# A position bias from an unscaled table: the maximum takes the constant, the eviction gives it back

## The chip, the cores and the metric

The kernel runs on one core of one Trainium2 chip. The metric is device time in microseconds (us), from repeated executions on the same chip; a further execution was recorded by the hardware profiler, and all rows below come from that one. The engines are TensorE (PE; PEld for its weight loads), VectorE (DVE), ScalarE (ACT), GpSimd (POOL) and SyncE (SP), which issues the DMAs.

## The reference

Attention with a learned relative-position bias, and two feed-forward layers behind it. Cut to what the change touches:

```python
pos = np.arange(S)                                        # S = 576
rel = (pos[:, None] - pos[None, :]).astype(np.float32)
psi_rel = np.log1p(np.abs(rel))
psi_i = np.log1p(np.maximum(pos[:, None].astype(np.float32), 1.0))
x = (psi_rel / psi_i)[..., None]
h = np.maximum(x @ w1 + b1, 0.0)                          # 32 hidden units
bias = h @ w2                                             # 8 heads
scores = scores + bias.transpose(2, 0, 1)[None, :, :, :]
# softmax, values; then silu(x @ w_gate) * (x @ w_val) @ w_out, then softplus(x @ w_in) @ w_out
```

psi_i is positive, so max(psi_rel / psi_i * w1 + b1, 0) = max(psi_rel * w1 + b1 * psi_i, 0) / psi_i. Both kernels use this: the inner maximum is computed per hidden unit, multiplied by w2, and the division by psi_i (with the factor 8 of the score scale) is done when the result is evicted.

## The kernel before

The program has three parts, one behind the other: the bias stage, attention, and the two feed-forward layers. The first is the one that the change touches.

**Table.** One input, `G`, holds 128 rows (32 hidden units for each of four row groups): the columns `wb_sb` (w1 and b1 of the row's hidden unit), `W2` (w2 laid out for four groups of rows), `PB` (psi_i, 36 slabs x 4 parts), a near and a far table of log-distances, and `inv` (8 / psi_i for each slab). It comes in two DMAs: everything up to the near table, then the far table and `inv`.

**Slabs.** The bias of 576 rows x 576 columns x 8 heads is made in 36 slabs; `order` says that slabs 32 to 35 (near table) come first, then 0 to 31 (far table). For one slab `hidden` makes four tiles `r` of 128 x 576, one per part `ct`: a window of the table, plus the part's bias, and the maximum with 0. Three are made by VectorE (one instruction with an add and a maximum, L267), the fourth by ScalarE (a Relu with a bias, L265). In the first slab two of the four are made by ScalarE, straight from the unscaled table with w1 as scale (L261). `second` multiplies the four tiles by `W2` on TensorE into a PSUM tile `pb` of 128 x 576 (eight matmuls of 288 columns, one per part and half, L275). `keep` evicts it with ScalarE, times `inv`, into a staging tile (L287), and SyncE sends it to its place in `bias` (L291, L294).

**Scaling.** Before the slabs VectorE multiplies `PB` by b1 in place (L604) and the near table by w1 into a tile `N` (L605); ScalarE multiplies the far table by w1 in place (L607).

**Order.** PE, ACT, DVE, POOL and SP run each in the order in which the code issues (a manual schedule). `hidden` runs two slabs ahead of `second`; there are 12 `r` tiles (three slabs) and two `pb` tiles. After slabs 23, 26, 31 and 33 (`EARLY`) the first attention chunks are run between slabs: two or four score matmuls (L311), a score-plus-bias with a row minimum on VectorE (L359), an exponential on ScalarE (L373). All other attention chunks stand behind the last slab. Ten warm-up matmuls (L602) stand ahead of the first slab on TensorE.

Of the kernel before, what the change touches and what calls it, by code (L numbers as in the profile page):

```python
# [11 lines left out]
F32 = mybir.dt.float32  # L12
F32R = mybir.dt.float32r
I32 = mybir.dt.int32
AF = mybir.ActivationFunctionType
ALU = mybir.AluOpType
# [3 lines left out]
P = 128  # L20
B, H, S, D, HID = 2, 8, 576, 64, 32
# [28 lines left out]
HALF = S // 2  # L50
# [3 lines left out]
GU0, GW = 487, 487 + S + 1  # L54
TU0, TW = 563, 51 + S + 1
# [48 lines left out]
def tile_kernel(ctx: ExitStack, tc, qT, kT, vS, vT, wg, wv, wo, wi, wo2, table, out):  # L104
    nc = tc.nc
# [11 lines left out]
    def slots(pool, tag, names):  # L117

        for name in names:
            n = len([1 for t in SLOTS.values() if t[0] == tag])  # L120
            SLOTS[name] = (tag, [pool.tile([P, 2, S], F32R, tag=f"{tag}{2 * n + i}", name=f"{name}{t}") for i, t in enumerate("hl")])

    def opener(stack):
        return lambda name, bufs, **k: stack.enter_context(
            tc.tile_pool(name=name, bufs=bufs, reuse_waits="tile", **k)
        )

    rctx = ExitStack()
    with ExitStack() as actx:
        pool = opener(actx)  # L130
        biasp = pool("biasp", 1)
        bias = [biasp.tile([P, H, S], F32, name=f"bias{c}") for c in range(2)]
# [19 lines left out]
        def new_pairs(name, count, pool=pool, **k):  # L152

            ep = pool(name, 1, **k)
            for _ in range(count):
                pairs.append(ep.tile([P, 2 * S], F32, name=f"e{len(pairs)}"))
            return ep
# [5 lines left out]
        psS = pool("psS", 2, space=PSUM)  # L163
# [73 lines left out]
        gp = pool("gp", 1)  # L237
# [1 line left out]
        psB = pool("psB", 2, space=PSUM)  # L239

        G = gp.tile([P, 34 + 144 + TW + GW + 36], F32, name="G")
        N = gp.tile([P, TW], F32, name="N")
        near = 34 + 144
        cut = near + TW
        sp.dma_start(out=G[:, :cut], in_=table[:, :cut])
        sp.dma_start(out=G[:, cut:], in_=table[:, cut:])
        wb_sb, W2, PB, inv = G[:, :2], G[:, 2:34], G[:, 34:near], G[:, cut + GW :]

        def hidden(i):
            s = order[i]  # L250
            c, t = divmod(s, 8)
            rs = []
            for ct in range(4):
                if c < 4:
                    src, w0 = G, cut + GU0 - (P * c + 32 * ct + t)
                else:
                    src, w0 = N, TU0 - (P * c + 16 * ct + t)
                r = rp.tile([P, S], F32, name="r")
                n = 4 * s + ct
                if i == 0 and ct > 1:  # L260
                    nc.scalar.activation(  # L261
                        r, G[:, near + w0 : near + w0 + S], AF.Relu, bias=PB[:, n : n + 1], scale=wb_sb[:, 0:1]
                    )
                elif ct == 3:
                    nc.scalar.activation(r, src[:, w0 : w0 + S], AF.Relu, bias=PB[:, n : n + 1])  # L265
                else:
                    nc.vector.tensor_scalar(r, src[:, w0 : w0 + S], PB[:, n : n + 1], 0.0, op0=ALU.add, op1=ALU.max)  # L267
                rs.append(r)
            return rs

        def second(rs):
            pb = psB.tile([P, 2, 512], F32, tag="B", name="pb")
            for hf in range(2):
                for ct in range(4):
                    nc.tensor.matmul(  # L275
                        pb[32 * ct : 32 * ct + 32, hf, :HALF],
                        W2,
                        rs[ct][:, HALF * hf : HALF * (hf + 1)],
                        start=True,
                        stop=True,  # L280
                    )
            return pb

        def keep(s, pb):
            c, t = divmod(s, 8)
            st = next(staging)
            nc.scalar.activation(  # L287
                st.rearrange("p (a n) -> p a n", a=2), pb[:, :, :HALF], AF.Copy, scale=inv[:, s : s + 1]
            )
            if c < 4:  # L290
                sp.dma_start(out=bias[c][t : t + 121 : 8], in_=st)  # L291
            else:
                for a in range(2):
                    sp.dma_start(out=bias[c][D * a + t : D * a + t + 61 : 4], in_=st[a::2])  # L294
# [304 lines left out]
        with tc.manual_schedule(engines={E.PE, E.Activation, E.DVE, E.Pool, E.SP}):  # L599
            warm = psS.tile([P, 2, 512], F32, tag="S", name="warm")  # L600
            for _ in range(WARM):
                nc.tensor.matmul(warm[:, 0, :P], ident, ident, start=True, stop=True)  # L602

            nc.vector.tensor_scalar(PB, PB, wb_sb[:, 1:2], None, op0=ALU.mult)  # L604
            nc.vector.tensor_scalar(N, G[:, near:cut], wb_sb[:, 0:1], None, op0=ALU.mult)  # L605
            hid = [hidden(i) for i in range(2)]
            nc.scalar.mul(G[:, cut : cut + GW], G[:, cut : cut + GW], wb_sb[:, 0:1])  # L607
            for i, s in enumerate(order):
                pb = second(hid.pop(0))
                if i + 2 < len(order):  # L610
                    hid.append(hidden(i + 2))
                keep(s, pb)
                if i in EARLY:
                    run_slot()
            sctx.close()
            slots(xp, "a", ("B11", "T1"))
            pool = opener(actx)
            ep1 = new_pairs("ep1", 4, opener(right), side="right")
            tmpp = pool("tmpp", 1)
            t2f = tmpp.tile([P, 2, S], F32, name="t2f")  # L620
            for i, mp in enumerate((tmpp, ep1)):
                mixes.append(mp.tile([P, 5 * P], F32, name=f"m{i}"))
                nc.gpsimd.memset(mixes[-1][:, S:], 0.0)
            atp = pool("atp", 6)
            fp = pool("fp", 1)
            psT = pool("psT", 3, space=PSUM)
            psO = pool("psO", 1, space=PSUM)
            while slot < len(chunks) or jobs or turned or gathered or done or late or waiting:
                run_slot()
# [447 lines left out]
    with tc.manual_schedule(engines={E.PE}):  # L1077
        quads = {"z": z}
        for q in range(4):
# [5 lines left out]
            for word in f"{OTHER if q else FIRST} {TAIL}".split():  # L1085
                who, what = word
                if who in "tu":
                    n = int(what)
                    if ws is None:
                        ws = convert(first + 2, outs[0]) + convert(first + 3, outs[1])  # L1090
                    if q == 3 and n == 4:
                        t = TOKENS[n][0]
                        a = acc[t // 2][:, t % 2]
                        for at in (slice(0, DM // 2), slice(DM // 2, DM)):
                            if who == "t":
                                held[n, at.start] = wide()[:, 0]
                            ps = held[n, at.start]
# [9 lines left out]
                    for i, t in enumerate(TOKENS[n]):  # L1107
                        if who == "t":
                            continue
                        a, ps = acc[t // 2][:, t % 2], held[n][:, i]  # L1110
# [57 lines left out]
```

## Time and profile before

| | |
|---|---|
| median of 3 runs | 587.25 us (587.23 to 587.41) |
| profiled execution | 587.23 us |
| its span, first to last instruction | 585.5 us |
| busy, share of the span | PE 98%, PEld 86%, DVE 78%, ACT 64%, POOL 17% |
| mean granted TensorE clock | 1.00 |

Busy shares are averages over stages with different limits. The bias stage takes roughly the first tenth of the span; which engine is full there is read from a view of that stage alone. A busy time that includes overlap counts an instruction from its start to its end, though the next may start earlier, so a pace is read from start to start.

### The profile page before, as it was taken

What the parts mean: (1) busy time and instruction counts of PE and PEld (TensorE: products, weight loads), DVE (VectorE), ACT (ScalarE), POOL (GpSimd) and SP (SyncE); (2) the same over time, 40 slices, a digit from 0 to 9 for tenths busy, and PEclk for the clock granted to TensorE, in tenths of its full rate; (3) what the DMA queues carried; (4) which work ended last, traced back from release to release, by engine and by line L of the source; (5) the groups of instructions that cost most, each with busy time, mean ns of one, the idle gap of its engine ahead of it and who ended that gap; (6) DMA issues with size and microseconds to landing.
All of it is one profiled execution on the core that took longest, in us unless ns stands there. A gap on an engine that the chain in (4) does not pass through costs nothing.

```text
span 585.5 us, 11330 instructions
## 1 busy us (share of the span) xinstructions
PE 574.0 (98%) x4282; PEld 504.9 (86%) x4282; DVE 454.4 (78%) x971; ACT 375.1 (64%) x713; POOL 99.1 (17%) x151
## 2 busy tenths in 40 slices
PE   8999999999999999999999999999999999999997
PEld 5334588888887999999999999999989989988986
DVE  7999688888988998977879626579998876983432
ACT  7999888888787857656567325359726725733520
POOL 1002578888871000000000000000000000000000
PEclk9999999999999999999999999999999999999999
DMA  8999633233233342332343231322254241310012
GB/s 314 214 208 214 153 100 118 85 107 113 72 112 112 103 143 73 109 109 73 108 129 126 72 109 45 104 99 69 86 160 123 74 143 28 118 36 1 2 50 112
DMA packets 42039, 63.32 MB, mean 108 GB/s; under 512 B 4096, under 2 KB 30976, under 8 KB 41984
## 3 DMA queue, kind: packets, MB, share of 16 engines
q1 hardware_dynamic: 41984, 62.59, 36.2%
q8 instruction: 34, 0.56, 0.4%
q14 instruction: 21, 0.17, 0.1%
HBM read 49.60 MB, written 2.36 MB: 89 GB/s over the span
## 4 chain that ended last, share of the span: by engine, by line
PE 85%; DVE 6%; ACT 5%; DMA 2%; POOL 1%; issue 1%; DVEq 0%; POOLq 0%; ACTq 0%
PE pw L756 38%; PE pw L1064 17%; PE pw L707 13%; PE po L437 6%; PE pt L410 4%; PE ps L338 4%; ACT early L287 2%; ACT r L265 2%; PE ps L311 2%; PE pb L275 2%; DVE e L359 1%; DMA bias<-early 1%; DVE r L267 1%; DVE bias L359 1%; DVE T1l L457 1%
## 5 line engine op out<-in xcount | busy, mean ns | idle before, releaser
L1064 PE MATMUL pw<-oh,g2h 128*128 128x512 f32 (+1 forms) x148 | 56.9, 384 | 0.0
L1064 PE MATMUL pw<-oh,g2l 128*128 128x512 f32 (+1 forms) x148 | 56.9, 384 | 0.0
L1064 PE MATMUL pw<-ol,g2h 128*128 128x512 f32 (+1 forms) x148 | 56.8, 384 | 0.0
L707 PE MATMUL pw<-gl,sh 128*128 128x384 f32 x144 | 48.2, 335 | 0.0
L707 PE MATMUL pw<-gh,sl 128*128 128x384 f32 x144 | 48.2, 334 | 0.0
L707 PE MATMUL pw<-gh,sh 128*128 128x384 f32 x144 | 48.2, 334 | 0.0
L681 DVE SCALAR_TENSOR_TENSOR x<-raw,x 128x512 int32<-128x512 int32 x68 | 46.2, 687 | 0.9
L275 PE MATMUL pb<-r,G 128*32 128x288 f32 x576 | 42.7, 412 | 4.0 <-ACT early L287 1.4
L383 POOL TENSOR_SCALAR e<-e,sm 128x576 f32<-128x576 f32 x44 | 34.2, 788 | 65.2 <-DVE sm L380 49.0
L267 DVE TENSOR_SCALAR r<-G 128x576 f32<-128x576 f32 x96 | 42.0, 517 | 0.0
L359 DVE CUSTOM_DVE_ANT_0 e<-ps,bias 128x576 f32<-128x576 f32 x44 | 33.0, 750 | 11.5 <-PE ps L338 6.5
L275 PEld LDWEIGHTS pb<-r,G 128*32 128x32 f32 x576 | 16.8, 109 | 28.9 <-ACT early L287 17.1
L417 ACT COPY at<-pt 128x512 f32<-128x512 f32 (+2 forms) x69 | 36.4, 549 | 6.5 <-PE pt L410 6.1
L338 PE MATMUL ps<-kst,ql 128*128 128x288 f32 x120 | 36.9, 336 | 1.4 <-DVE sm L377 0.6
L437 PE MATMUL po<-at,v 128*64 128x256 f32 (+3 forms) x384 | 37.2, 332 | 1.0 <-DVE at L417 0.8
L373 ACT ACTIVATE e<-e,sm 128x576 f32<-128x576 f32 x44 | 34.3, 781 | 3.5 <-DVE sm L359 3.1
L678 DVE TENSOR_SCALAR x<-x 128x512 int32<-128x512 int32 x68 | 28.7, 427 | 9.4 <-ACT x L677 5.2
L1114 DVE TENSOR_TENSOR acc<-pw,acc 128x512 f32<-128x512 f32 x26 | 16.8, 684 | 23.7 <-PE pw L1064 23.7
L437 PEld LDWEIGHTS po<-at,v 128*64 128x64 f32 x384 | 26.8, 137 | 8.5 <-issue 1.7
L1064 PEld LDWEIGHTS pw<-oh,g2l 128*128 128x128 f32 x148 | 27.8, 188 | 5.7
L1064 PEld LDWEIGHTS pw<-ol,g2h 128*128 128x128 f32 x148 | 27.8, 188 | 5.1
L1064 PEld LDWEIGHTS pw<-oh,g2h 128*128 128x128 f32 x148 | 27.8, 188 | 5.0
(274 smaller groups left out, 1677.9 us busy)
## 6 DMA issues: line engine op xcount, KB each, us to landing
raw<-in_wo_dram SPq DMA_DIRECT2D x28, 512.0 KB, 3.4
bias<-early SPq DMA_DIRECT2D x32, 288.0 KB, 7.5
raw<-in_wi_dram SPq DMA_DIRECT2D x16, 512.0 KB, 4.1
raw<-in_wv_dram SPq DMA_DIRECT2D x12, 512.0 KB, 4.5
raw<-in_wg_dram SPq DMA_DIRECT2D x12, 512.0 KB, 3.5
qr<-in_qT_dram SPq DMA_DIRECT2D x7, 576.0 KB, 3.8
bias<-in_kT_dram SPq DMA_DIRECT2D x6, 576.0 KB, 4.5
v<-in_vS_dram SPq DMA_DIRECT2D x8, 384.0 KB, 3.3
```

The lines of the kernel that those rows point to most:

```text
L267: nc.vector.tensor_scalar(r, src[:, w0 : w0 + S], PB[:, n : n + 1], 0.0, op0=ALU.add, op1=ALU.max)
L275: nc.tensor.matmul(pb[32 * ct : 32 * ct + 32, hf, :HALF], W2, rs[ct][:, HALF * hf : HALF * (hf + 1)], start=True, stop=True,)
L338: nc.tensor.matmul(ps[:, hf, :HALF], u[t][:, o : o + P], kst[:, a, HALF * hf : HALF * (hf + 1)], start=i == 0, stop=i == len(parts) - 1,)
L359: nc.vector.tensor_tensor_reduce(out=e[:, :S].rearrange("p (a n) -> p a n", a=2), in0=ps[:, :, :HALF], in1=bt.rearrange("p (a n) -> p a n" ...
L373: nc.scalar.activation(e, e, AF.Exp, bias=sm[:, 0, n : n + 1], scale=-1.0, accum_out=u["sums"][:, n, :1])
L383: nc.gpsimd.tensor_scalar(e, e, sm[:, 2, i : i + 1], 1.0, op0=ALU.mult, op1=ALU.mult)
L417: marks[eng, u["i"], u["sub"]] = copy(at[:, :w], pt[:, :w]).ins
L437: nc.tensor.matmul(u["po"][D * a : D * (a + 1), o : o + n], v[:, D * t : D * (t + 1)], at[:, i : i + n], start=piece == 0 and o == 0, stop ...
L681: nc.vector.scalar_tensor_tensor(yi, lw, 29, yi, op0=ALU.logical_shift_right, op1=ALU.bitwise_or)
L707: nc.tensor.matmul(ps[:, :n], w[:, k], x, start=first and k == 0 and i == 0, stop=last and k == NK - 1 and i == 2)
L756: nc.tensor.matmul(ps[:, hf, :HALF], a[:, o + k], b[:, HALF * hf : HALF * (hf + 1)], start=start and k == 0 and i == 0, stop=k == 1 and i ...
L1064: nc.tensor.matmul(ps[:, at], g, w.rearrange("p k f -> p (k f)")[:, at], start=f == 0 and i == 0, stop=f == 3 and i == 2)
```

## The change

The table is no longer scaled ahead of the slabs. With a table entry g and a part's bias b = b1 * psi_i, the kernel before computes max(g * w1 + b, 0). The changed kernel computes max(g * w1, -b) in VectorE for three of the parts, which is smaller by b; the missing b, multiplied by `W2` and `inv`, is added in the eviction. `floor` holds -b for the three parts and 0 for the fourth; `edge` holds b for the fourth, whose Relu on ScalarE takes bias and scale. `shifts` multiplies `floor` by `W2` in four matmuls of 36 columns and turns the result into `shift`, one number per row and slab, which becomes the bias of the eviction (now Identity with a bias and a scale instead of Copy with a scale). The tile `N`, the scaling of both tables and the special case of the first slab are gone.

```diff
         G = gp.tile([P, 34 + 144 + TW + GW + 36], F32, name="G")
-        N = gp.tile([P, TW], F32, name="N")
+        floor = gp.tile([P, 36, 4], F32, name="floor")
+        edge = gp.tile([P, 36], F32, name="edge")
+        shift = gp.tile([P, 36], F32, name="shift")
...
+        PB = G[:, 34:near].rearrange("p (s c) -> p s c", c=4)
+        nc.gpsimd.memset(floor[:, :, 3], 0.0)
 
         def hidden(i):
...
                 r = rp.tile([P, S], F32, name="r")
-                n = 4 * s + ct
-                if i == 0 and ct > 1:
-                    nc.scalar.activation(
-                        r, G[:, near + w0 : near + w0 + S], AF.Relu, bias=PB[:, n : n + 1], scale=wb_sb[:, 0:1]
-                    )
-                elif ct == 3:
-                    nc.scalar.activation(r, src[:, w0 : w0 + S], AF.Relu, bias=PB[:, n : n + 1])
+                g, w1 = G[:, w0 : w0 + S], wb_sb[:, 0:1]
+                if ct == 3:
+                    nc.scalar.activation(r, g, AF.Relu, bias=edge[:, s : s + 1], scale=w1)
                 else:
-                    nc.vector.tensor_scalar(r, src[:, w0 : w0 + S], PB[:, n : n + 1], 0.0, op0=ALU.add, op1=ALU.max)
+                    nc.vector.tensor_scalar(r, g, w1, floor[:, s, ct : ct + 1], op0=ALU.mult, op1=ALU.max)
                 rs.append(r)
             return rs
+
+        def shifts():
+
+            ps = psS.tile([P, 2, 512], F32, tag="S", name="ps")
+            for ct in range(4):
+                nc.tensor.matmul(ps[32 * ct : 32 * ct + 32, 0, :36], W2, floor[:, :, ct], start=True, stop=True)
+            nc.vector.scalar_tensor_tensor(shift, ps[:, 0, :36], -1.0, inv, op0=ALU.mult, op1=ALU.mult)
...
             nc.scalar.activation(
-                st.rearrange("p (a n) -> p a n", a=2), pb[:, :, :HALF], AF.Copy, scale=inv[:, s : s + 1]
+                st.rearrange("p (a n) -> p a n", a=2),
+                pb[:, :, :HALF],
+                AF.Identity,
+                bias=shift[:, s : s + 1],
+                scale=inv[:, s : s + 1],
             )
...
-            nc.vector.tensor_scalar(PB, PB, wb_sb[:, 1:2], None, op0=ALU.mult)
-            nc.vector.tensor_scalar(N, G[:, near:cut], wb_sb[:, 0:1], None, op0=ALU.mult)
+            nc.vector.tensor_scalar(
+                floor[:, :, :3], PB[:, :, :3], wb_sb[:, 1:2], -1.0, op0=ALU.mult, op1=ALU.mult
+            )
+            nc.scalar.mul(edge, PB[:, :, 3], wb_sb[:, 1:2])
             hid = [hidden(i) for i in range(2)]
-            nc.scalar.mul(G[:, cut : cut + GW], G[:, cut : cut + GW], wb_sb[:, 0:1])
+            shifts()
             for i, s in enumerate(order):
```

ScalarE's queue from its first table instruction on, in the kernel before (`r` are the hidden tiles, `early` the staging tiles of the eviction, `pb` the PSUM tile of a slab):

```order
L261 ACTIVATE r<-G 128x576 x2
L265 ACTIVATE r<-N,G 128x576
L607 ACTIVATE G<-G 128x1064
L265 ACTIVATE r<-N,G 128x576
L287 ACTIVATE early_120<-pb,G 128x576
L265 ACTIVATE r<-N,G 128x576
L287 ACTIVATE early_120<-pb,G 128x576
```

Two Relus with bias and scale, one Relu, the scaling of the far table and one more Relu stand ahead of the first eviction there. The same place in the changed kernel, where `edge` and `shift` are the new operands:

```order
L620 ACTIVATE edge<-G 128x36
L267 ACTIVATE r<-G,edge 128x576 x3
L296 ACTIVATE early_120<-pb,shift,G 128x576
L267 ACTIVATE r<-G,edge 128x576
L296 ACTIVATE early_120<-pb,shift,G 128x576
L267 ACTIVATE r<-G,edge 128x576
```

The scaling of the table and one Relu are gone from ahead of the first eviction, and the small `edge` stands first; Relu and eviction alternate as before. VectorE's queue from its start to the first attention chunk, in the kernel before (`e` is that chunk's score tile):

```order
L604 TENSOR_SCALAR G<-G 128x144
L605 TENSOR_SCALAR N<-G 128x628
L267 TENSOR_SCALAR r<-N,G 128x576 x11
L267 TENSOR_SCALAR r<-G 128x576 x66
L359 ISA e_115,sm_100<-ps,bias_71 128x576
```

Two scalings stand ahead of 77 maxima. The same place in the changed kernel:

```order
L617 TENSOR_SCALAR floor<-G 128x36x3
L269 TENSOR_SCALAR r<-G,floor 128x576 x6
L278 SCALAR_TENSOR_TENSOR shift<-ps,G 128x36
L269 TENSOR_SCALAR r<-G,floor 128x576 x72
L372 ISA e_115,sm_100<-ps,bias_71 128x576
```

One small instruction (`floor`) stands ahead of 78 maxima, and the shift stands behind the sixth of them, where it waits for TensorE's four small products. On TensorE these four stand between the warm-up matmuls and the first slab. The order of the DMAs on SP is the same.

## Rows read from the trace of the kernel before

**Rows 1.** The page's chain that ended last, share of the span by engine.

```profile
PE 85%; DVE 6%; ACT 5%; DMA 2%; POOL 1%; issue 1%; DVEq 0%; POOLq 0%; ACTq 0%
```

**Rows 2.** Chain of waits in order of time: start us, us, what.

```profile
55.11 0.74 ACT early L287
...
188.50 126.71 PE pw L756 x960
```

**Rows 3.** Busy time of each engine in two stretches of the bias stage.

```profile
core 0: us, PE busy (x) PEld busy (x) DVE busy (x) ACT busy (x) POOL busy (x), PEclk, DMA share, GB/s
...
9.00:37.00 28.00, 25.52 (x352) 9.15 (x352) 28.00 (x67) 28.00 (x44) 0.00 (x0) 1.00 1.03 235
37.00:57.00 20.00, 18.92 (x228) 8.67 (x220) 18.59 (x50) 19.50 (x34) 2.83 (x5) 1.00 1.05 213
```

**Rows 4.** Timeline of ScalarE: start us, us, engine line op out<-in xcount [idle before].

```profile
4.24 1.62 ACT L261 ACTIVATE r<-G 128x576 f32<-128x576 f32 x2 [2.23 <-DVE G L604]
...
5.78 0.76 ACT L265 ACTIVATE r<-N,G 128x576 f32<-128x576 f32 x1
...
6.44 1.17 ACT L607 ACTIVATE G<-G 128x1064 f32<-128x1064 f32 x1
...
8.18 0.72 ACT L287 ACTIVATE early<-pb,G 128x576 f32<-128x576 f32 x1
8.81 0.76 ACT L265 ACTIVATE r<-N,G 128x576 f32<-128x576 f32 x1
...
37.88 0.83 ACT L287 ACTIVATE early<-pb,G 128x576 f32<-128x576 f32 x1
```

**Rows 5.** Timeline of VectorE from its start to the first attention chunk.

```profile
3.91 0.30 DVE L604 TENSOR_SCALAR G<-G 128x144 f32<-128x144 f32 x1 [3.91 <-DMA G<-in_table_dram]
4.12 0.54 DVE L605 TENSOR_SCALAR N<-G 128x628 f32<-128x628 f32 x1
4.70 4.81 DVE L267 TENSOR_SCALAR r<-N,G 128x576 f32<-128x576 f32 x11
9.43 28.43 DVE L267 TENSOR_SCALAR r<-G 128x576 f32<-128x576 f32 x66
```

**Rows 6.** Timeline of TensorE: two slabs at the start, two later (half-matmuls counted).

```profile
5.94 2.21 PE L275 MATMUL pb<-r,G 128*32 128x288 f32 x32
...
41.97 2.15 PE L275 MATMUL pb<-r,G 128*32 128x288 f32 x32
```

**Rows 7.** Relus of L261 and L265: duration ns min/median/max, first and last start.

```profile
L261 ACT ACTIVATE r<-G x2: 852/860/867, 4.2 to 5.0; 128x576 f32<-128x576 f32 x2
...
L265 ACT ACTIVATE r<-N,G x3: 759/760/762, 5.8 to 8.8; 128x576 f32<-128x576 f32 x3
```

**Rows 8.** Timeline of ScalarE in the feed-forward part: casts and copies without operands.

```profile
305.77 1.25 ACT L686 CAST gh<-g 128x576 fp32r<-128x576 f32 x2
...
309.80 0.63 ACT L785 COPY pw<-pw 128x576 f32<-128x576 f32 x1
310.37 0.66 ACT L675 ACTIVATE x<-raw 128x512 f32<-128x512 f32 x1
```

**Rows 9.** Timeline of VectorE: a small instruction, and one with constants only.

```profile
54.62 0.17 DVE L380 RECIPROCAL sm<-sm 128x2 f32<-128x2 f32 x1
...
301.07 0.43 DVE L678 TENSOR_SCALAR x<-x 128x512 int32<-128x512 int32 x1
301.41 0.75 DVE L827 TENSOR_TENSOR g<-pw,gate 128x576 f32<-128x576 f32 x1
```

**Rows 10.** ScalarE from 37.88 to 55.10 us by line: xcount, busy us, mean ns.

```profile
L287 ACT ACTIVATE early<-pb,G 128x576 f32<-128x576 f32 x12 | 9.0, 746 | 0.1
L265 ACT ACTIVATE r<-G 128x576 f32<-128x576 f32 x11 | 8.7, 791 | 0.0
L373 ACT ACTIVATE e<-e,sm 128x576 f32<-128x576 f32 x3 | 2.3, 777 | 0.0
L373 ACT ACTIVATION_READ_ACCUMULATOR e<-e,sm 128x1 f32 x3 | 0.6, 203 | 0.0
```

More of the change, by code (lines that the diff above doesn't have):

```diff
@@ L246, in tile_kernel @@
         sp.dma_start(out=G[:, cut:], in_=table[:, cut:])
-        wb_sb, W2, PB, inv = G[:, :2], G[:, 2:34], G[:, 34:near], G[:, cut + GW :]
+        wb_sb, W2, inv = G[:, :2], G[:, 2:34], G[:, cut + GW :]
+        PB = G[:, 34:near].rearrange("p (s c) -> p s c", c=4)
+        nc.gpsimd.memset(floor[:, :, 3], 0.0)
         def hidden(i):
@@ L254, in hidden @@
                 if c < 4:
-                    src, w0 = G, cut + GU0 - (P * c + 32 * ct + t)
+                    w0 = cut + GU0 - (P * c + 32 * ct + t)
                 else:
-                    src, w0 = N, TU0 - (P * c + 16 * ct + t)
+                    w0 = near + TU0 - (P * c + 16 * ct + t)
                 r = rp.tile([P, S], F32, name="r")
-                n = 4 * s + ct
-                if i == 0 and ct > 1:
-                    nc.scalar.activation(
-                        r, G[:, near + w0 : near + w0 + S], AF.Relu, bias=PB[:, n : n + 1], scale=wb_sb[:, 0:1]
-                    )
-                elif ct == 3:
-                    nc.scalar.activation(r, src[:, w0 : w0 + S], AF.Relu, bias=PB[:, n : n + 1])
+                g, w1 = G[:, w0 : w0 + S], wb_sb[:, 0:1]
+                if ct == 3:
+                    nc.scalar.activation(r, g, AF.Relu, bias=edge[:, s : s + 1], scale=w1)
                 else:
-                    nc.vector.tensor_scalar(r, src[:, w0 : w0 + S], PB[:, n : n + 1], 0.0, op0=ALU.add, op1=ALU.max)
+                    nc.vector.tensor_scalar(r, g, w1, floor[:, s, ct : ct + 1], op0=ALU.mult, op1=ALU.max)
                 rs.append(r)
             return rs
+        def shifts():
[3 more added lines that the diff above has]
+            nc.vector.scalar_tensor_tensor(shift, ps[:, 0, :36], -1.0, inv, op0=ALU.mult, op1=ALU.mult)
         def second(rs):
```

## The prediction

> **What bounds the kernel now.** I read the chain of waits first, by engine and then in order of time. Over the whole span it is 85% TensorE [rows 1], and from 188.50 us on it is an unbroken run of matmuls [rows 2]. So this change, which touches only the bias stage, can move the time in one way: by moving the moment at which that stage hands over to attention. The chain leaves the bias stage at ScalarE's last eviction, at 55.11 us [rows 2]. Everything behind it depends on it in turn (scores, exponentials, transposes, values), and I saw no piece in it that waits for a fixed hour, so I carry a shift of the last eviction 1:1 to the end.
>
> Next the busy time by stretch: from 9 to 37 us VectorE is busy 28.00 of 28.00 us and ScalarE 28.00 of 28.00 [rows 3]. Both are full. The timelines say how. ScalarE does one Relu and one eviction for each of the 36 slabs; a Relu is followed by the next start after 0.66 us (5.78 to 6.44), an eviction after 0.63 (8.18 to 8.81), together 1.29 [rows 4]. From the first eviction (8.18) to the 24th (37.88) are 23 slabs in 29.70 us, 1.291 each. VectorE does three maxima a slab: 11 of them from 4.70 to 9.43, 0.430 each, three in 1.29 [rows 5]. Two engines with the same pace, neither with slack: whatever makes either one's instruction longer is paid in all 36 slabs. TensorE has room: two slabs run in 2.15 us when nothing holds them, 1.08 a slab [rows 6].
>
> **The change, part by part.** The change removes the passes that scaled the tables (L605 and L607 of before) and pays by giving every per-slab instruction one more per-partition operand. Before, VectorE's maximum reads one (the bias) beside the constant 0; after, it reads two (w1 and the floor). ScalarE's Relu reads a bias before, a bias and a scale after. The eviction reads a scale before, a scale and a bias after. The instruction counts per slab stay the same.
>
> *Relu with two operands.* The trace has this very form: the two L261 Relus at the start take a bias and a scale. They last 852 and 867 ns, where the Relu with a bias alone lasts 760 [rows 7]. In pace: the two start at 4.24 and the next Relu at 5.78, 0.77 each against 0.66 [rows 4]. So +0.105 us a slab.
>
> *Eviction with two operands.* No row has it. Below: nothing, as if the second read hid. Above: the Relu's +0.105. The nearest rows for a source in PSUM: a copy with no per-partition operand lasts 0.63 and the next starts after 0.57 (309.80 to 310.37) [rows 8], the eviction with one lasts 0.72 and the next starts after 0.63. The first operand so cost 0.09 in length and 0.06 in pace. On the Relu's side a cast with none runs at 1.25 us for two [rows 8], 0.58 in pace, so the first operand cost 0.09 there and the second 0.105: the second was no cheaper than the first. I take +0.10: an eviction every 0.73. ScalarE's slab is then 0.77 + 0.73 = 1.50 instead of 1.29, +0.205.
> The Trainium skill, "ScalarE: Activation LUTs", section "What ACT_TABLE_LOAD costs", adds about 93 ns for each such operand and lets neighbours overlap by as much; an estimate from that page makes the slab 1.48, and the stage 0.7 us shorter than mine. The Relu rows agree with it; the eviction with both is not in this trace.
>
> *Maximum with two operands.* No row has it. Below: nothing. Above: ScalarE's 0.105, the dearest second operand in the trace. The nearest price is that of VectorE's own first operand. L604 (144 elements, 0.30 us) and L605 (628, 0.54) both have one [rows 5]; that is 0.50 ns per element. At 512 elements a maximum's pace of 0.430 becomes 0.40. A tensor-scalar instruction of 512 elements with constants only is followed by the next start after 0.34 (301.07 to 301.41) [rows 9]. So the first operand cost 0.06, and I take 0.06 for the second: 0.49 each, 1.47 a slab.
>
> *Start.* ScalarE loses one two-operand Relu (0.77) and L607 (6.44 to the next start 1.08) and gains the edge multiply. That is 36 elements; I estimate 0.3 from the 0.30 of L604. It starts at 3.91, when the first table piece lands, and ScalarE, after three Relus of 0.77, is ready to evict at about 6.6. It is not let: behind the warm-up TensorE is free at 5.94 [rows 6], the four tiny products (an estimate of 0.4, they are short but each loads weights) and the first slab (1.1) follow, so 7.5. GpSimd's memset of the floor's fourth column, for which the fourth product waits, stands behind GpSimd's other memsets while the table is still being loaded: nothing, and if it came late, the products would move by no more than its own length. VectorE's shift stands behind the floor (0.3) and six maxima (2.6 to 2.9), and takes some 0.2 (a two-element reciprocal takes 0.17 [rows 9]), so 7.1 to 7.5. The second table piece is there by then: L607 read it at 6.44 without a wait. First eviction at about 7.6 instead of 8.18: -0.6.
>
> *Sum on ScalarE.* Start -0.6. To the 24th eviction 23 x 0.205 = +4.7. From there to the last, 17.23 us before: 12 evictions, 10 whole Relus (an eleventh reaches in from the left) and 3 exponentials [rows 10], 12 x 0.63 + 10 x 0.665 + 3 x 0.76 (pace with the accumulator read, an estimate from 0.78 and 0.20 less the overlaps) = 16.5, so 0.7 us of waiting. After, 12 x 0.73 + 10 x 0.77 + 2.3 = 18.8: +1.5 if all that waiting is eaten up, +2.3 if none. Sum +5.6 to +6.4.
> *Sum on VectorE.* Floor instead of L604 and L605: 0.35 instead of 0.79, -0.45. One maximum more (ScalarE made it before), +0.49. Shift +0.2. The other 107 maxima x 0.06 = +6.4. Sum +6.6. What cover there was for VectorE is gone: its queue holds maxima and the early score reductions in one order, so each delay reaches these too.
> The later engine sets the end, and they come out within a microsecond of each other. I take +6.4 on the profiled execution, 587.23 us (span 585.5), which lies 0.02 under the median of the runs: 593.6. From below, that one number holds within 1 us whether ScalarE or VectorE is the last.
>
> **Rivals.**
> *VectorE's second operand is free.* Its sum is then -0.45 + 0.43 + 0.2 = +0.2, and ScalarE alone decides: +5.6 to +6.4, 593.2. For it: VectorE could fetch both in one go, and nothing here shows two. Against: its first was not free.
> The Trainium skill, "VectorE: DVE Perf Modes", section on the TRN2 errata, gives the cost of an instruction as a fixed 58 cycles plus its elements, with no term for operands; by that rule the second is free and this rival holds. The trace speaks against the rule already for the first: 0.43 in pace at 576 elements, where the page comes to 0.36 (estimate).
> *Only the Relu pays.* With the eviction's second operand and VectorE's at nothing, ScalarE's slab is 0.77 + 0.63 = 1.40, 35 x 0.11 = +3.7, less 0.6 at the start and some 0.5 of the waiting: +2.6, 589.8.
> *The operand fetch hides: not slower.* Late in the stage a Relu and an eviction overlap far more than early (the eviction at 37.88 lasts 0.83, the one at 8.18 0.72, at the same pace [rows 4]). If the longer instruction only starts earlier and the pace stays 1.29, the start's -0.6 on ScalarE meets VectorE's +0.2, and VectorE decides: 587.4; if the shift is cheaper than I think, 586.8. The point from which this decides is 0.6 / 35 = 0.02 us of added pace per slab. Against it: the L261 rows show 0.105 in pace, not in length alone.
> *VectorE's second operand costs 0.10*, as ScalarE's does: 107 x 0.10 + 0.3 = +11, 598.2.
> *TensorE's clock drops.* TensorE would be busy 1.08 of 1.50 us instead of 1.08 of 1.29. At the 1.2 GHz level a slab takes 2.16, so 35 x 0.87 = +30, 617. Against it: granted clock 1.00 (2.4 GHz) in both stretches of this stage [rows 3], also where TensorE waits longer.
>
> **How the numbers follow.** Both engines pay: 0.55, 593.6. VectorE free: 0.25, 593.2. Only the Relu: 0.06. VectorE dear: 0.06. Clock: 0.03. Hidden: 0.05. The first two fill 592.4 to 594.8 by the two sums; intermediate prices of VectorE's operand (up to 0.08) and of the eviction's (down to 0.05) widen it to 591.0 to 596.0, and the other four cases, 0.20, lie outside. A measurement of this kernel tells about 0.2%, 1.2 us, from no change. All cases but the hidden one are slower by more: 0.95; that one I split 0.03 same, 0.02 faster.
>
> **What would show it.** In the profile after: Relu near 860 ns and eviction near 820 to 830 in length; evictions 1.48 to 1.51 us apart between the first and the 24th; VectorE's maxima about 0.57 long at a pace of 0.49, or still 0.43 with gaps where it waits for free buffers (then the first rival). First eviction near 7.6, last near 61.5, the first matmul of the long run near 195. The forecast is wrong if the evictions still come 1.29 apart, if VectorE's slab is over 1.55, if the granted clock leaves 1.00, or if the last eviction moves by 6 us and the end doesn't.

## The result, and the profile after

The changed kernel takes 593.75 us (median of 4 runs, 593.69 to 593.81), the kernel before beside it 587.33 us (587.23 to 587.41): a ratio of 1.0109, 95% interval 1.0094 to 1.0124, so 6.4 us slower. The profiled execution has a span of 592.0 us, against 585.5.

The chain of waits of the changed kernel, in order of time, beside [rows 2]:

```profile
61.40 0.83 ACT early L296
...
195.02 126.77 PE pw L771 x960
```

The last eviction starts 6.29 us later than before (55.11), the unbroken run of matmuls 6.52 us later (188.50), and that run itself lasts 126.77 us against 126.71. So 6.29 of the 6.5 us by which the span grew are made in the bias stage; attention adds 0.23, and nothing behind it gives any back.

Timeline of ScalarE in the changed kernel (start us, us, engine line operation out<-in), beside [rows 4]:

```profile
3.97 0.36 ACT L620 ACTIVATE edge<-G 128x36 f32<-128x36 f32 x1 [1.95 <-DMA G<-in_table_dram]
...
4.36 2.39 ACT L267 ACTIVATE r<-G,edge 128x576 f32<-128x576 f32 x3
...
7.97 0.83 ACT L296 ACTIVATE early<-pb,shift,G 128x576 f32<-128x576 f32 x1 [1.23 <-PE pb L284]
8.71 0.86 ACT L267 ACTIVATE r<-G,edge 128x576 f32<-128x576 f32 x1
...
9.47 0.82 ACT L296 ACTIVATE early<-pb,shift,G 128x576 f32<-128x576 f32 x1
10.18 0.86 ACT L267 ACTIVATE r<-G,edge 128x576 f32<-128x576 f32 x1
...
41.92 0.89 ACT L296 ACTIVATE early<-pb,shift,G 128x576 f32<-128x576 f32 x1
```

The Relu lasts 0.86 us instead of 0.76, the eviction 0.82 instead of 0.72. From the second eviction (9.47) to the 24th (41.92) are 22 slabs in 32.45 us: 1.475 each, where it was 1.291.

Timeline of VectorE in the changed kernel, beside [rows 5]:

```profile
3.97 0.28 DVE L617 TENSOR_SCALAR floor<-G 128x108 f32<-128x108 f32 x1 [3.97 <-DMA G<-in_table_dram]
4.28 3.03 DVE L269 TENSOR_SCALAR r<-G,floor 128x576 f32<-128x576 f32 x6
7.22 0.19 DVE L278 SCALAR_TENSOR_TENSOR shift<-ps,G 128x36 f32<-128x36 f32 x1
7.33 35.38 DVE L269 TENSOR_SCALAR r<-G,floor 128x576 f32<-128x576 f32 x72
```

72 maxima in 35.38 us, without a gap: 0.49 from start to start, where it was 0.43. Three make 1.475. So in the changed kernel, too, two engines have the same pace, and the views by stretch show both full, with TensorE's clock as it was [rows 3]:

```profile
9.00:37.00 28.00, 22.66 (x308) 8.97 (x308) 28.00 (x58) 28.00 (x39) 0.00 (x0) 1.00 0.86 233
```

The columns are those of [rows 3]: after the stretch and its length come the busy times of PE, PEld, DVE, ACT and POOL, then the granted clock. With two full engines one profile can't say which of them makes the loss, or whether one is full only because it waits inside its instructions for the other. That is what the experiments are for.

### The profile page after: what moved, and what is told of

It reads as the page before. It is cut to its first block, busy times and chain, and to the rows that moved or that the text cites. A ratio compares the mean times of both kernels' runs of the same rounds, so it can differ in the third digit from the quotient of the medians.

```text
span 592.0 us, 11346 instructions
## 1 busy us (share of the span) xinstructions
PE 577.5 (98%) x4290; PEld 506.7 (86%) x4290; DVE 460.1 (78%) x972; ACT 380.0 (64%) x712; POOL 98.9 (17%) x152
## 4 chain that ended last, share of the span: by engine, by line
PE 85%; DVE 6%; ACT 5%; issue 1%; POOL 1%; DMA 1%; DVEq 0%; POOLq 0%; ACTq 0%
PE pw L771 38%; PE pw L1079 17%; PE pw L722 13%; PE po L450 6%; PE pt L423 4%; PE ps L351 4%; ACT early L296 3%; PE pb L284 2%; ACT r L267 2%; PE ps L324 1%; DVE e L372 1%; DVE r L269 1%; PE warm L615 1%; DVE bias L372 1%; DVE T1l L470 1%
## 5 line engine op out<-in xcount | busy, mean ns | idle before, releaser
L269 DVE TENSOR_SCALAR r<-G,floor 128x576 f32<-128x576 f32 x108 | 53.8, 582 | 0.0
L284 PE MATMUL pb<-r,G 128*32 128x288 f32 x576 | 45.8, 415 | 6.8 <-ACT early L296 6.8
L284 PEld LDWEIGHTS pb<-r,G 128*32 128x32 f32 x576 | 18.3, 110 | 33.3 <-ACT early L296 21.0
```

What stands on the lines that cost most here:

```text
L269: nc.vector.tensor_scalar(r, g, w1, floor[:, s, ct : ct + 1], op0=ALU.mult, op1=ALU.max)
L284: nc.tensor.matmul(pb[32 * ct : 32 * ct + 32, hf, :HALF], W2, rs[ct][:, HALF * hf : HALF * (hf + 1)], start=True, stop=True,)
```

## The experiments

The kernel before took 587.18 us (median) beside each of the first seven kernels.

### VectorE back to one operand

```diff
-                    nc.vector.tensor_scalar(r, g, w1, floor[:, s, ct : ct + 1], op0=ALU.mult, op1=ALU.max)
+                    nc.vector.tensor_scalar(r, g, 1.0, floor[:, s, ct : ct + 1], op0=ALU.mult, op1=ALU.max)
```

> The changed kernel with VectorE's maximum reading one per-partition operand (the floor) and the constant 1.0 in w1's place, so the product with w1 is left out of three parts. ScalarE keeps two operands in Relu and eviction. Theory (each second operand lengthens its own engine's pace, either engine alone is enough): VectorE back to 0.430 a maximum, ScalarE still 0.76 + 0.72 a slab, evictions 1.47 to 1.48 apart, 592.7 to 593.7 us. Rival V (VectorE sets the pace, ScalarE's second operands hide in the overlap of neighbours): evictions 1.29 apart, 587.2 to 588. Rival S (ScalarE alone sets the pace): as the theory, 593.7.

Measured: 592.65 us, ratio 1.0090 (1.0075 to 1.0105), 5.5 us slower than before; that is 0.05 below the range expected, and the four executions lie between 591.77 and 593.01. Busy time by stretch (columns as in [rows 3]), and ScalarE's timeline:

```profile
9.00:36.00 27.00, 21.59 (x296) 7.76 (x300) 25.71 (x58) 27.00 (x37) 0.00 (x0) 1.00 0.92 233
```

```profile
9.56 0.82 ACT L296 ACTIVATE early<-pb,shift,G 128x576 f32<-128x576 f32 x1
10.28 0.86 ACT L267 ACTIVATE r<-G,edge 128x576 f32<-128x576 f32 x1
...
40.54 0.88 ACT L296 ACTIVATE early<-pb,shift,G 128x576 f32<-128x576 f32 x1
```

VectorE is no longer full (25.71 of 27.00), ScalarE is, and 21 slabs take 30.98 us, 1.475 each: 0.72 for the eviction (9.56 to 10.28) and 0.76 for the Relu. ScalarE's second operands make most of the loss by themselves. Rival V is out.

### ScalarE back to one operand

```diff
-                    nc.scalar.activation(r, g, AF.Relu, bias=edge[:, s : s + 1], scale=w1)
+                    nc.scalar.activation(r, g, AF.Relu, bias=edge[:, s : s + 1])
...
-                AF.Identity,
-                bias=shift[:, s : s + 1],
+                AF.Copy,
                 scale=inv[:, s : s + 1],
```

> The changed kernel with one operand in each ScalarE instruction: the Relu without the scale w1 and the eviction a Copy with scale, without the shift (shift is still computed); the product with w1 in the fourth part and the added shift are left out. VectorE keeps two operands. Theory: VectorE's 0.49 a maximum makes a slab of 1.475 by itself, 593.2 to 593.9 us. Rival V: the same, 593.7. Rival S (ScalarE alone sets the pace, VectorE's second operand is hidden or only shows because it waits): evictions 1.29 apart, 587.2 to 588, VectorE's pace back to 0.43.

Measured: 593.55 us, ratio 1.0108 (1.0091 to 1.0125), 6.4 us slower. By stretch, and VectorE's timeline:

```profile
9.00:36.00 27.00, 27.00 (x301) 11.13 (x301) 27.00 (x56) 25.87 (x38) 0.00 (x0) 1.00 1.00 241
```

```profile
7.29 35.37 DVE L269 TENSOR_SCALAR r<-G,floor 128x576 f32<-128x576 f32 x72
```

Now ScalarE has gaps (25.87 of 27.00), VectorE has none, and its 72 maxima take 35.37 us, to 0.01 us the time of the changed kernel. Rival S is out as well: the 0.49 is VectorE's own and no wait for ScalarE. Each engine alone makes the loss or most of it; together they don't make it twice: 5.5 and 6.4 alone, 6.4 in the changed kernel.

### One operand everywhere, with the new start

Both edits above together.

> Both edits of the two runs before together: one operand everywhere, but the changed kernel's start (floor, edge, four tiny products, shift, no scaled tables). The products with w1 and the shift are left out. Theory: slab 1.29 again; VectorE's start saves 0.45 us and pays 0.43 for a maximum and 0.2 for the shift, so 587.2 to 587.8 us. Rival (the four products, the shift and what waits for them are part of the loss): 588.5 or more, with the first eviction not earlier than the 8.18 of before. Rival (the start is a gain that the operands ate up): 586.7 or less.

Measured: 586.98 us, ratio 0.9997 (0.9988 to 1.0006): no difference from before that can be told. It lies 0.2 below the theory's range and above that of the second rival. The first eviction starts at 7.80 us instead of 8.18, so the first rival is out as well, and VectorE is back at 0.43 a maximum (ScalarE's and VectorE's timeline):

```profile
7.80 0.74 ACT L296 ACTIVATE early<-pb,G 128x576 f32<-128x576 f32 x1 [1.44 <-PE pb L284]
```

```profile
6.86 31.00 DVE L269 TENSOR_SCALAR r<-G,floor 128x576 f32<-128x576 f32 x72
```

The loss is gone. What the new start costs (the floor, the four tiny products, the shift, one more maximum) and what it saves (the scaling passes) come to nothing that can be measured, taken together; no run has one without the other. The loss comes with the operands.

### A second operand put into the kernel before

```diff
+        zero = gp.tile([P, 1], F32, name="zero")
+        nc.gpsimd.memset(zero, 0.0)
...
-                    nc.vector.tensor_scalar(r, src[:, w0 : w0 + S], PB[:, n : n + 1], 0.0, op0=ALU.add, op1=ALU.max)
+                    nc.vector.tensor_scalar(r, src[:, w0 : w0 + S], PB[:, n : n + 1], zero, op0=ALU.add, op1=ALU.max)
```

> The kernel before with one change: the constant 0 of VectorE's maximum is a per-partition operand that holds zeros. Nothing is left out, and no other instruction changes. Theory: 107 maxima x 0.06 = 6.4, so 593.5 to 593.9 us, maxima about 0.58 long at a pace of 0.49, evictions 1.47 apart, though ScalarE's instructions have one operand each. Rival S: 587.2 to 588. Rival M (not the second operand costs, but the multiply or reading the floor tile): VectorE's pace stays 0.43, 587.3.

Measured: 593.51 us, ratio 1.0107 (1.0092 to 1.0122). VectorE's timeline:

```profile
10.22 32.44 DVE L269 TENSOR_SCALAR r<-G,zero 128x576 f32<-128x576 f32 x66
```

32.44 us for the 66 maxima that took 28.43 [rows 5], 0.061 more each. The same numbers are computed by the same operations; only the zero is fetched per partition instead of standing in the instruction. On VectorE this one operand costs what the whole change costs, in a kernel without the multiply, the floor and the new eviction, so on this engine it is none of these.

### ScalarE's two operands one by one

Both kernels have VectorE's maximum with the constant 1.0. One keeps the eviction's second operand and drops the Relu's, the other the reverse.

> The changed kernel with a second operand in the eviction alone: the maximum has the constant 1.0 in w1's place and the Relu no scale; the product with w1 is left out in all parts. Theory (each second operand adds its own price to ScalarE's slab): 0.665 + 0.717 = 1.38 a slab, evictions 1.38 apart, 589.2 to 590.2 us. Rival (one of ScalarE's two does it all, the other hides): 587.0 to 587.5 or 592.3 to 592.9. Eviction about 820 ns long at first, Relu 760.

> The changed kernel with a second operand in the Relu alone: the maximum has the constant 1.0 in w1's place and the eviction is a Copy with scale, without the shift; the product with w1 in three parts and the shift are left out. Theory: 0.76 + 0.63 = 1.39 a slab, evictions 1.39 apart, 589.2 to 590.4 us; with the run of the eviction alone the rises add up to that of both (5.5). Rival as there: 587.0 to 587.5 or 592.3 to 592.9.

Measured: 589.30 us, ratio 1.0035 (1.0023 to 1.0048), with the eviction's; 588.44 us, ratio 1.0025 (1.0015 to 1.0035), with the Relu's, which is 0.8 below the range given. ScalarE's timeline, the second and the 24th eviction, first of the kernel with the eviction's second operand:

```profile
9.16 0.82 ACT L296 ACTIVATE early<-pb,shift,G 128x576 f32<-128x576 f32 x1
...
39.57 0.89 ACT L296 ACTIVATE early<-pb,shift,G 128x576 f32<-128x576 f32 x1
```

and of the one with the Relu's:

```profile
8.44 0.73 ACT L296 ACTIVATE early<-pb,G 128x576 f32<-128x576 f32 x1
...
38.83 0.80 ACT L296 ACTIVATE early<-pb,G 128x576 f32<-128x576 f32 x1
```

22 slabs in 30.41 us and in 30.39: 1.382 and 1.381. Each operand adds 0.091 to the slab, and both add 0.184 (1.475 against 1.291): the pace is the sum. With its second operand the eviction also becomes an Identity instead of a Copy, and no run has an Identity with one operand; that the Relu, whose function stays, pays the same 0.091 speaks for the operand, but for the eviction alone it isn't shown. The times are not the sum: 2.1 and 1.3 us alone, 5.5 together (the first experiment). In the profiles the 24th to the last eviction, where ScalarE had some 0.7 us of waiting to give, explains a part (+0.5 and +0.2 us, where twelve slabs of 0.091 more would be +1.1), and the start another: the Relu's kernel evicts first at 7.04 us, the other at 7.76. TensorE's timeline, of the one with the Relu's and of the other:

```profile
5.60 0.32 PE L277 MATMUL ps<-floor,G 128*32 128x36 f32 x8
5.72 3.49 PE L284 MATMUL pb<-r,G 128*32 128x288 f32 x46
```

```profile
6.08 0.35 PE L277 MATMUL ps<-floor,G 128*32 128x36 f32 x8
6.22 3.12 PE L284 MATMUL pb<-r,G 128*32 128x288 f32 x40
```

In that execution TensorE came to the tiny products half a microsecond earlier. The ten warm-up matmuls in front took 4.16 us there and 4.63 in the other; in the kernel before they took 4.49 and in the run with `zero`, where the same ten stand first on TensorE, 4.02. So this time varies from profile to profile, and the nine executions of the Relu's kernel lie between 588.20 and 589.30 us. What makes it vary was not studied. As far as the profile shows, the miss in the time lies in this start, not in the pace.

### Can idle GpSimd take some of the work

If operands can't be saved, instructions could be moved: GpSimd does nothing between its memsets and the first softmax product.

```diff
+                elif i > 3 and (i % 3, ct) in ((0, 2), (1, 3)):
+                    nc.gpsimd.tensor_scalar(r, src[:, w0 : w0 + S], PB[:, n : n + 1], 0.0, op0=ALU.add, op1=ALU.max)
                 elif ct == 3:
```

> The kernel before with GpSimd, idle in this stage, making every twelfth hidden tile in VectorE's place and every twelfth in ScalarE's from the fifth slab on (21 tiles), one operand each; nothing is left out. If GpSimd runs beside VectorE for free: VectorE's slab falls by 0.14 and ScalarE's by 0.22 on average, some 32 x 0.14 = 4.5 us, 582.5 to 583.5. If it holds VectorE up as the early softmax product at 43.95 us did in the kernel before (1.19 us long where others last 0.75, and five maxima beside it in 2.63 instead of 2.23): VectorE saves 11 x 0.43 = 4.7 and loses 21 x 0.4 = 8.4, so 590 to 592. I expect the second.

Measured: 602.14 us, ratio 1.0256 (1.0241 to 1.0271). Slower as expected, but by four times as much, so the reason given was not the main one (and ten of the 21 tiles were VectorE's, not 11). The hidden tiles by line (xcount, duration ns min/median/max):

```profile
L265 POOL TENSOR_SCALAR r<-G x21: 2258/2617/6383, 8.7 to 64.7; 128x576 f32<-128x576 f32 x21
L269 DVE TENSOR_SCALAR r<-G x86: 503/516/999, 9.5 to 67.7; 128x576 f32<-128x576 f32 x86
```

A hidden tile takes GpSimd 2.62 us (2.75 on average, with one of 6.38), where its softmax product of the same size takes 0.75. GpSimd makes two for each three slabs, one behind the other: 1.75 a slab instead of 1.29. For 32 slabs that makes 14.5 us (an estimate), nearly all of the 15.0 lost. VectorE's maxima last 0.51 as before or, 38 of those that run while GpSimd works, 0.6 to 1.0. Two more runs (one execution each) asked whether the form of GpSimd's instruction or VectorE beside it makes the 2.62:

```diff
-                    nc.gpsimd.tensor_scalar(e, e, sm[:, 2, i : i + 1], 1.0, op0=ALU.mult, op1=ALU.mult)
+                    nc.gpsimd.tensor_scalar(e, e, sm[:, 2, i : i + 1], 0.0, op0=ALU.mult, op1=ALU.max)
```

> The kernel before with GpSimd's softmax product (mult, mult by 1) written as mult and max with 0; the products are not negative, so nothing changes in the result. It asks why GpSimd's hidden tiles took 2.75 us each in the run that shared the maxima, where its products take 0.75. Theory F (the form with a maximum is slow on GpSimd): these 72 instructions last over 1.5 us each and the time rises by many us, since attention waits for them. Theory C (GpSimd was held up by VectorE's maxima beside it): they stay at 0.75 and the time at 587.2.

> The same with mult and add of 0. Theory F with the add as the slow step: over 1.5 us each. Theory C: 0.75 us each and 587.2.

Measured: 664.13 us with the maximum, 587.29 with the add (587.36 before, beside them). In the first of these TensorE waited more (busy 91% of the span, not 98%) and its mean granted clock was 0.96 (between the levels of 1.2 and 2.4 GHz), so the rise may hold more than GpSimd's own time. The softmax products by line (duration ns min/median/max), with the maximum and with the add:

```profile
L383 POOL TENSOR_SCALAR e<-e,sm x44: 2195/2206/2892, 43.9 to 257.0; 128x576 f32<-128x576 f32 x44
```

```profile
L383 POOL TENSOR_SCALAR e<-e,sm x44: 740/752/1185, 43.9 to 178.6; 128x576 f32<-128x576 f32 x44
```

The maximum makes the instruction three times as long on GpSimd, the add does not. Theory F holds for 2.2 of the 2.62 us; the rest, and VectorE's long maxima, fit the two engines holding each other up, which was not separated further. As the hidden tiles need a maximum, GpSimd is no help here.

## Why the prediction was right

The mechanism held: both engines pay for a second operand in each instruction, the handover moves, and the end moves with it (6.29 us at the last eviction, 6.5 at the end). The slabs of the two engines came out equal, 1.475, where 1.50 and 1.47 were forecast. Forecast 593.6, measured 593.75. Point by point:

- *Relu with two operands:* forecast 0.77 in pace, measured 0.76. The two Relus at the start of the kernel before [rows 7] had shown it; 0.105 was read from starts given to 0.01 us, and over 22 slabs it is 0.091.
- *Eviction with two operands:* no row had it, and 0.73 was taken; it is 0.72, and 0.091 is the price here as well. ScalarE's slab so is 1.475 and not 1.50, close to the 1.48 estimated from the Trainium skill ("ScalarE: Activation LUTs", section "What ACT_TABLE_LOAD costs", about 93 ns for each such operand); the two runs that add one operand each agree with it.
- *Maximum with two operands:* taken at 0.49, from the price of the first operand. Measured 0.49, and 0.061 for the operand in the kernel before. That the price fits so well is in part luck: the row with constants only [rows 9] is a shift of whole numbers with one operation (L678), no row or run has the maximum with constants only, and so the price of its first operand isn't shown. The first rival, VectorE's second operand free, fell with this, and with it the rule of the Trainium skill that it was worked out beside ("VectorE: DVE Perf Modes", section on the TRN2 errata: fixed cycles plus elements, no term for operands; the section says itself that this row comes out low for single instructions): here the trace decides against it, 0.43 and 0.49 for the same elements.
- *Start:* forecast -0.6, measured -0.2 (7.97 against 8.18). The edge and three Relus were done at 6.74 (6.6 forecast), and the tiny products, for which the prediction had no row, took 0.35 (0.4 estimated). The eviction then waited 1.23 us for TensorE, whose first slab, from 6.23 on, took longer than the 1.1 that were put down. The trace of the changed kernel shows it stopping twice for no wait that the profile knows:

```profile
6.69 0.20 PEld L284 LDWEIGHTS pb<-r,G 128*32 128x32 f32 x4 [0.28 <-issue]
...
7.16 1.09 PEld L284 LDWEIGHTS pb<-r,G 128*32 128x32 f32 x20 [0.27 <-issue]
```

- *To the 24th eviction:* forecast +4.7, measured +4.25 (33.95 us against 29.70), by the 0.02 in the slab. *From there to the last:* forecast +1.5 to +2.3, measured +2.25 (19.48 against 17.23). These sum to 6.3, so the two small errors, a start that gained less by 0.4 and slabs that were shorter by 0.45 in all, cancelled: that ScalarE's sum comes out so close is luck.
- *Which engine is last:* the sums were 5.6 to 6.4 for ScalarE and 6.6 for VectorE. Alone, ScalarE's operands cost 5.5 and VectorE's 6.4, and the changed kernel 6.4: the later of the two, VectorE. Late in the stage ScalarE shows the waits for it, through TensorE; first ScalarE's timeline, then TensorE's waits up to 62 us (us in total, times, longest):

```profile
51.92 0.83 ACT L296 ACTIVATE early<-pb,shift,G 128x576 f32<-128x576 f32 x1 [0.20 <-PE pb L284]
...
61.40 0.83 ACT L296 ACTIVATE early<-pb,shift,G 128x576 f32<-128x576 f32 x1 [0.50 <-PE pb L284]
```

```profile
PEld pb L284 <- DVE r L269: 3.0, 9, 0.5
```

In the run in which ScalarE alone pays, these waits of TensorE come to 0.7 us, ScalarE waits for none of its evictions late in the stage, and from the 24th to the last are 18.48 us, 1.25 more than before. The +2.25 of the changed kernel so holds about 1 us of waiting for VectorE, and it meets the upper end of ScalarE's sum by chance.

- *Rivals:* "only the Relu pays" and "the fetch hides" are refuted by the pace of each run; the granted clock stayed at 1.00; the dear operand of VectorE (0.10) did not show.

## What to carry to other kernels

An operand that is read per partition has a price of its own in each instruction (here 0.06 us on VectorE, 0.09 on ScalarE, on instructions of 0.4 to 0.8 us), so a pass over a table that is folded into the instructions that read it has to be weighed against the operands that they read for it: two passes of 1.7 us together were saved here, and some 180 operands bought. Where two engines are full at the same pace, as here, neither price hides, the later engine sets the loss, and undoing one half of such a change gives little back (0.9 us of 6.4 for VectorE's half, nothing that can be told for ScalarE's). Read paces from start to start over many instructions, since one gap of a trace is only good to a hundredth or two.

## What was not expected

GpSimd's tensor-scalar instruction with a maximum takes 2.2 us on 128x576 where the one with two products, or a product and a sum, takes 0.75.

On ScalarE the recorded length showed in these runs whether it had to wait: at a constant pace the eviction's length crept from 0.82 to 0.88 us in the run in which ScalarE alone was full, and stayed at 0.74 in the one in which it waited for others, the first and the later eviction of which follow:

```profile
7.54 0.74 ACT L296 ACTIVATE early<-pb,G 128x576 f32<-128x576 f32 x1 [1.12 <-PE pb L284]
...
40.99 0.74 ACT L296 ACTIVATE early<-pb,G 128x576 f32<-128x576 f32 x1
```

It doesn't tell which engine is the later: in the changed kernel it crept as well, to 0.89 at 41.92, and was back at 0.83 at 51.92, behind a wait. In the kernel before it crept from 0.72 to 0.83 [rows 4], which the prediction read as a point for the hidden fetch; it creeps with one operand and with two, so it is no sign of that. What makes it grow no run shows.
